# All remainder key tiles at the start of a visit: moving norms, loads and turned pairs forward in a fused attention and MLP kernel

## The chip, the cores and the metric

The kernel runs on one NeuronCore of a Trainium2 chip, as one launch. The metric is the device time of one execution in microseconds (us). TensorE (PE in the profile) multiplies matrices, ScalarE (ACT) applies functions, VectorE (DVE) does elementwise work, GpSimd (POOL) does squares and issues some DMAs, and SyncE (SP) issues the other DMAs, one after the other in the order of the program.

## The reference

```python
# q, k, v: [8 batches, 12 heads, 448 rows, 64]; tau = 0.1
q_n = q / (norm(q) + 1e-6);  k_n = k / (norm(k) + 1e-6)
attn = softmax(q_n @ k_n.T / tau);  o = attn @ v
x = o.transpose(0, 2, 1, 3).reshape(8 * 448, 768)   # heads side by side
h = x @ w_in                     # [3584, 2048]
out = max(0.01 * h, h) @ w_out   # [3584, 768]
```

## The kernel before

**Pairs.** The heads of a batch are taken two at a time: six pairs a batch, 48 pairs in all, numbered s. For a pair, `load_qk(s)` (L135) issues four DMAs on SP: two of 192 KB for rows 0 to 383 of q and of k, and two small ones for the 64 remainder rows. `squares(s)` (L171) squares them on POOL, `sums(s)` (L184) reduces them on DVE, `roots(s)` (L195) takes Ln and Exp on ACT, and `normalise(s)` (L211) divides on DVE and leaves bf16 `qn[s]`. `transposes(s)` (L246) then turns `qn[s]`, so that the head dimension lies on the partitions: `qkT[s]`, here called the turned pair. From pair 10 on this is one transposing DMA on SP (L252); before, PE and DVE do it. `norm(s)` (L690) is the bundle: roots, normalise, the turn, the load of a later pair (s + 4), a small copy `hold` on POOL (L509) that makes POOL wait for `qn[s]`, and the squares of pair s + 2.

**Key tiles.** `key_tiles` (L265) multiplies the keys of a pair with its queries. A pair has three full tiles of 128 key rows (ki = 0 to 2). The 64 remainder rows of two neighbouring pairs share one more tile (ki = 3), named by the odd pair of the two; it reads both turned pairs. So a batch has 18 full tiles and three remainder tiles: pairs 0 and 1, 2 and 3, 4 and 5. Each takes two of the eight PSUM banks until ACT has taken the exponent of it (L289) into `pe` (full) or `pr` (remainder).

**Stages.** After a start-up for batch 0 the loop at L759 runs over chunks b = 0 to 7 of token rows, with 384 rows in even chunks and 512 in odd ones. For each of them:

1. *visit b* (`visit`, L718) multiplies chunk b by w_out, in `groups` (L437) of three or four blocks of 128 rows, and deals out the 21 key tiles of batch b + 1 between the steps of it. A step is one pair of half-depth matmuls that run side by side; a block has 32 steps. The dictionaries `three`, `four` and `wide` (L735 to L737) say after which step how many tiles come. Two remainder tiles stand ahead of the first block (L723), the third behind the last (L733).
2. `attend_batch(b + 1)` (L679) forms softmax sums and products with v for the three pairs of pairs, two of these together (`attend_two`) and then one (`attend`), and scales them into `xT`.
3. `firsts(b + 1, ...)` (L708), here the *first stage* of chunk b + 1, multiplies by w_in: 16 slices m of six matmuls each, 384 columns wide in even chunks and 512 in odd ones. Each is followed on ACT by the leaky ReLU into `hT` (L388).

PE thus goes visit 1, attend 2, first stage 2, visit 2 and so on, and only the last chunk has no key tiles.

**What sets the order.** All of it is written by hand: each engine takes its instructions in the order in which the program names them. The dictionaries `norms` (by block and step in a visit) and `between` (by m in a first stage) name the places of the norms and sums. `ready` counts the pairs whose norms are placed. A visit's batch need not be all turned at its start: a pair is turned at the latest shortly before its own tiles come. With batch b + 1 due in visit b, the last two or three pairs of the batch have their norms in the visit itself.

**Buffers.** raw q and k of the first six pairs and of pairs 10 and 11 lie in `raw0`; the others rotate through four `ld` buffers. Turned pairs rotate through five `qt` buffers. The weights `w_out` come in four DMAs on POOL's queue, two behind `norm(6)` and two behind `norm(7)`.

Of the kernel before, what the change touches and what calls it, by code (L numbers as in the profile page):

```python
# [8 lines left out]
F32 = mybir.dt.float32  # L9
# [7 lines left out]
def kernel(  # L17
# [11 lines left out]
    B, H, S, D = q.shape  # L29
# [7 lines left out]
    NPAIR = H // 2  # L37
    NSLOT = B * NPAIR
    NQ = NPAIR // 2
# [8 lines left out]

    ctx.enter_context(tc.manual_schedule())
    cpool = ctx.enter_context(tc.tile_pool(name="consts", bufs=1))  # L50
    ldp = ctx.enter_context(tc.tile_pool(name="ld", bufs=4))
    vbp = ctx.enter_context(tc.tile_pool(name="vb", bufs=4))
    sqp = ctx.enter_context(tc.tile_pool(name="sq", bufs=3))
    smp = ctx.enter_context(tc.tile_pool(name="small", bufs=3))
    qnp = ctx.enter_context(tc.tile_pool(name="qn", bufs=3))
    qtp = ctx.enter_context(tc.tile_pool(name="qt", bufs=5))
    pep = ctx.enter_context(tc.tile_pool(name="pe", bufs=6))
    prp = ctx.enter_context(tc.tile_pool(name="pr", bufs=3))
    rbp = ctx.enter_context(tc.tile_pool(name="rb", bufs=2))
# [50 lines left out]
    def load_w_out(parts):  # L110
        for m in parts:
            gp.dma_start(out=w_out_sb[:, m : m + MT // 4], in_=w_out_r[:, m : m + MT // 4])

    def main(x, b, h0, nh):
        return x[b, h0 : h0 + nh, 0:MAIN].rearrange("h (p t) d -> p h t d", t=3)

    raw0 = cpool.tile([128, NPAIR, 2, 7, D], F32, name="raw0")
    raw = {s: (raw0[:, s, :, 0:4], raw0[:, s, :, 4:7]) for s in range(NPAIR)}

    def load_first(eng, x, part, s0, n):  # L120

        h0, i = 2 * s0, 0 if x is q else 1
        if part == 0:
            dst = raw0[:, s0 : s0 + n, :, 4 * i : 4 * i + 3]
            eng.dma_start(
                out=dst.rearrange("p s h t d -> p (s h) t d"), in_=main(x, 0, h0, 2 * n)
            )
        else:
            dst = raw0[64 * i : 64 * i + 64, s0 : s0 + n, :, 3]
            eng.dma_start(  # L130
                out=dst.rearrange("p s h d -> p (s h) d"),
                in_=x[0, h0 : h0 + 2 * n, MAIN:S].rearrange("h p d -> p h d"),
            )

    def load_qk(s):  # L135
        if s >= NSLOT:
            return
        b, h0 = s // NPAIR, 2 * (s % NPAIR)
        both = raw0[:, s - 10] if s in (10, 11) else ldp.tile([128, 2, 7, D], F32, name="qk")
        nc.sync.dma_start(out=both[:, :, 0:3], in_=main(q, b, h0, 2))  # L140
        nc.sync.dma_start(out=both[:, :, 4:7], in_=main(k, b, h0, 2))
        for i, x in enumerate((q, k)):
            nc.sync.dma_start(
                out=both[64 * i : 64 * i + 64, :, 3],
                in_=x[b, h0 : h0 + 2, MAIN:S].rearrange("h p d -> p h d"),
            )
        raw[s] = (both[:, :, 0:4], both[:, :, 4:7])
# [117 lines left out]
    def key_tiles(which):  # L265

        tiles = []
        for s, ki in which:
            sc = banks(2)
            tiles.append(sc)  # L270
            for i in range(2 if ki == 3 else 1):
                x = qkT[s - 1 + (i ^ s // 2 % NQ % 2)] if ki == 3 else qkT[s]
                for a in range(2):
                    rows = slice(64 * a, 64 * a + 64)
                    out = sc[64 * i : 64 * i + 64] if ki == 3 else sc
                    c0, c1 = (448, 512) if ki == 3 else (512 + 128 * ki, 640 + 128 * ki)
                    nc.tensor.matmul(  # L277
                        out=out[:, a, :S], lhsT=x[rows, c0:c1], rhs=x[rows, 0:S],
                        start=True, stop=True,
                    )  # L280
        for (s, ki), sc in zip(which, tiles):
            if ki == 3:
                pr[s // 2] = prp.tile([128, 2, S], BF16, name="pr")
                dst = pr[s // 2]
            else:
                if s not in pe:
                    pe[s] = pep.tile([128, 3, 2, S], BF16, name="pe")
                dst = pe[s][:, ki]
            nc.scalar.activation(out=dst, in_=sc[:, :, :S], func=AF.Exp, scale=inv_tau)  # L289

    xT = {}
# [217 lines left out]
    def hold(x):  # L509
        seen = smp.tile([128, 1], F32, name="seen")  # L510
        gp.tensor_copy(out=seen, in_=x)  # L511

    hold(raw0[:, 0, 0, 3, 0:1])
    for x in (q, k):
        load_first(gp, x, 1, 3, 3)
    load_v(0)
# [23 lines left out]
    dst = qtp.tile([128, 7, 128], BF16, name="qkT")  # L540
# [137 lines left out]

    def attend_batch(b):  # L679
        if b == 1:  # L680
            load_qk(14)
            load_qk(15)
            sums(12)
        attend_two(b * NQ)
        if b == 1:
            norm(12)
        attend(b * NQ + 2)


    def norm(s, transposed=True):  # L690
        if s >= NSLOT:
            return
        roots(s)
        normalise(s)
        if transposed:
            transposes(s)
        if s == 10:
            return
        for x in (12, 13) if s == 11 else (s + 4,) if s > 11 else ():
            load_qk(x)  # L700
        hold(qn[s][:, 6, 0, 0:1])
        if s == 11:
            squares(12)
        squares(s + 2)
        if s in (6, 7):
            load_w_out((0, 4) if s == 6 else (8, 12))

    def firsts(b, begun, between):  # L708

# [8 lines left out]
    def visit(b, order, norms, between):  # L718


        s0 = (b + 1) * NPAIR
        tiles = [(s0 + p, ki) for p in range(NPAIR) for ki in range(3)]
        key_tiles([(s0 + 1, 3), (s0 + 3, 3)])  # L723
        for i, pairs in enumerate(order):
            last = i == len(order) - 1
            after = between[last]
            for n, _ in enumerate(groups(b, pairs, 4 if len(pairs) > 1 else 1, last), 1):
                for _ in range(after.get(n, 0)):
                    key_tiles([tiles.pop(0)])
                for fn in norms.get((i, n), ()):  # L730
                    fn()
        assert not tiles
        key_tiles([(s0 + 5, 3)])  # L733

    three = ({5: 1, 11: 1, 16: 2, 21: 1, 27: 1}, {3: 1, 7: 1, 11: 1, 16: 2, 20: 1})  # L735
    wide = (dict.fromkeys((5, 11, 16, 22, 27, 33, 38, 44, 49, 55, 60), 1), dict.fromkeys(range(4, 29, 4), 1))
    four = ({5: 1, 11: 1, 16: 2, 24: 1}, {6: 1, 16: 2})  # L737

    deals["apart"] = False
    attend(NQ - 1, [lambda m=m: first(0, m, range(KT - 2)) for m in range(3, SOON)])  # L740
    behind(nc.sync, scalings[NQ - 1, 0], "weights first")
    load_qk(10)
    load_qk(11)
    norm(6, False)
    norm(7, False)
    firsts(
        0, SOON, {
# [4 lines left out]
            11: [lambda: transposes(8), lambda: load_v(4)],  # L752
            13: [lambda: load_v(5), lambda: load_v_rem(1)],
            14: [lambda: transposes(9), lambda: sums(10)],
            15: [lambda: norm(10)],
        },
    )
    ready = 10
    for b in range(B):  # L759
        tokens = chunk_cols(b)[1] // 128  # L760
        if b == B - 1:
            for ts in range(tokens):
                for half in range(2):
                    second(b, ts, half)
            break
        order = [[((ts, 0), (ts, 1))] for ts in range(tokens)]
        if b == 0:
            order = [order[0] + order[1], order[2]]
        norms = {(0, 8): [lambda: sums(11)], (0, 18): [lambda: norm(11)]}
        if b:  # L770
            norms = {}
            for i in range(tokens - 1):
                norms[i, 4] = [lambda s=ready + i: norm(s)]
                norms[i, 20] = [lambda s=ready + i + 1: sums(s)]
        visit(b, order, norms, wide if b == 0 else three if tokens == 3 else four)
        ready += tokens - 1
        attend_batch(b + 1)
        for j in range((b + 2) * NQ, (b + 3) * NQ):
            load_v(j)
        load_v_rem(b + 2)  # L780
        s = ready
        between = {0: [lambda s=s: norm(s)], 1: [lambda s=s: sums(s + 1)]}
        if b == 0:
            between = {
                0: [lambda: sums(13)], 1: [lambda: norm(13), lambda: sums(14)],
                4: [lambda: norm(14), lambda: sums(15)], 7: [lambda: norm(15)],
                13: [lambda: sums(16)],
            }
            ready += 4
        elif tokens == 3:  # L790
            between.update({
                4: [lambda s=s: norm(s + 1), lambda s=s: sums(s + 2)],
                7: [lambda s=s: norm(s + 2), lambda s=s: sums(s + 3)],
                10: [lambda s=s: norm(s + 3)], 13: [lambda s=s: sums(s + 4)],
            })
            ready += 4
        else:
            between.update({
                4: [lambda s=s: norm(s + 1)], 5: [lambda s=s: sums(s + 2)],
                8: [lambda s=s: norm(s + 2)], 12: [lambda s=s: sums(s + 3)],  # L800
            })
            ready += 3
        firsts(b + 1, 0, between)


# [33 lines left out]
```

## Time and profile before

| | |
|---|---|
| median of 3 runs | 409.8 us (409.0 to 410.4) |
| the profiled execution | 409.4 us |
| its span, first to last instruction | 407.6 us |
| outside the span | 1.8 us |
| visit 1, with its 21 key tiles | 99.0 to 124.1 us |
| first stage 3 | 173.0 to 193.8 us |
| visit 3 | 193.8 to 218.8 us |

Busy shares of the span: PE 98%, ACT 65%, PEld 53%, DVE 47%, POOL 34%. "PEld" is the load of weights into TensorE, which overlaps the matmuls. Rows of the timeline give the start of a run of equal instructions, its length and how many there are; SPq is the sequencer of SP, whose rows are the issues of DMAs. The transfer itself goes on after the row's end until it lands.

### The profile page before, as it was taken

The page shows a single profiled execution, that of the slowest core. Times are in us where ns is not written, and L with a number is a line of the kernel's source. Part 1 is how long each engine was busy: PE and PEld are TensorE (multiplying, and loading weights), DVE is VectorE, ACT ScalarE, POOL GpSimd, SP SyncE. Part 2 cuts the span into 40 slices and gives each one's busy share as a digit, 9 for nine tenths or more (in the row PEclk, how much of TensorE's full clock was granted, in tenths as well). Part 3 has the DMA queues.
Part 4 walks back from the last instruction along what each step waited for, and adds up shares of the span by engine and source line. Part 5 has one row for each costly group of instructions (what it writes and reads, how often), then busy time and mean ns, then how long its engine had stood idle before and what let it go on. Part 6 is the DMA issues. An engine that isn't in the chain of part 4 may idle for free.

```text
span 407.6 us, 10141 instructions
## 1 busy us (share of the span) xinstructions
PE 399.9 (98%) x4096; PEld 215.1 (53%) x4096; DVE 189.6 (47%) x405; ACT 263.1 (65%) x454; POOL 138.7 (34%) x212
## 2 busy tenths in 40 slices
PE   7999999999999999999999999999999999999996
PEld 2335566544555655544555555544555555554564
DVE  6987941770644624354542635256261645130021
ACT  5996498565865589745876569845876559944300
POOL 4973842371323432253241614055231530000000
PEclk9999999999999999999999999999999999999999
DMA  7999999596497848377396957486378833210033
GB/s 187 247 214 240 202 200 223 160 192 120 107 189 127 146 82 216 65 117 179 71 168 149 130 121 165 111 117 145 84 177 157 111 75 63 63 41 2 0 78 78
DMA packets 102095, 54.21 MB, mean 133 GB/s; under 512 B 69984, under 2 KB 96992, under 8 KB 102048
## 3 DMA queue, kind: packets, MB, share of 16 engines
q1 hardware_dynamic: 78064, 41.04, 43.9%
q0 software_dynamic: 23136, 12.00, 22.4%
q8 instruction: 32, 0.52, 0.5%
q10 hardware_dynamic: 848, 0.52, 0.4%
q14 instruction: 15, 0.12, 0.1%
HBM read 45.61 MB, written 11.01 MB: 139 GB/s over the span
## 4 chain that ended last, share of the span: by engine, by line
PE 88%; DVE 5%; POOL 2%; ACT 1%; DMA 1%; issue 1%; POOLq 0%
PE ps L381 33%; PE ps L456 31%; PE ps L317 11%; PE ps L277 8%; PE ps L418 5%; DVE qn L220 2%; PE ps L304 1%; POOL sq L180 1%; DMA raw<-in_k_dram 1%; DVE ss L191 1%; DVE ss L215 1%; DVE qkT L258 1%; DVE r L216 0%; POOL raw L130 0%; POOL v_rem L165 0%
## 5 line engine op out<-in xcount | busy, mean ns | idle before, releaser
L381 PE MATMUL ps<-xT,w_in_sb 128*128 128x384 bf16 (+1 forms) x768 | 148.2, 353 | 0.0
L456 PE MATMUL ps<-w_out_sb,hT 64*128 64x384 bf16 x1536 | 143.4, 323 | 0.0
L289 ACT ACTIVATE pe<-ps 128x896 bf16<-128x896 f32 x144 | 124.0, 918 | 20.0 <-PE ps L277 18.0
L388 ACT ACTIVATE hT<-ps 128x384 bf16<-128x384 f32 (+1 forms) x128 | 67.4, 543 | 70.5 <-PE ps L381 70.2
L381 PEld LDWEIGHTS <-w_in_sb 128*128 128x128 bf16 x768 | 74.1, 98 | 71.9 <-issue 4.0
L456 PEld LDWEIGHTS <-hT 64*128 64x128 bf16 x1536 | 75.0, 94 | 53.9 <-PE ps L456 4.2
L180 POOL TENSOR_TENSOR sq<-qk 128x512 f32<-128x512 f32 x80 | 73.4, 938 | 10.7 <-DMA qk<-in_k_dram 10.1
L277 PE MATMUL ps<-qkT 64*128 64x448 bf16 (+1 forms) x384 | 54.9, 354 | 1.3 <-ACT pr L289 0.5
L468 DVE COPY osb<-ps 128x384 f32<-128x384 f32 x41 | 21.2, 553 | 74.6 <-PE ps L456 44.1
L511 POOL CAST seen<-qn 128x1 f32<-128x1 bf16 x47 | 8.8, 186 | 136.0 <-DVE qn L220 127.2
L191 DVE TENSOR_REDUCE ss<-sq 128x6 f32<-128x384 f32 (+1 forms) x95 | 54.4, 611 | 1.2 <-POOL sq L180 1.1
L220 DVE TENSOR_TENSOR qn<-qk,r 128x512 bf16<-128x512 f32 x80 | 48.2, 644 | 1.7 <-DVE r L216 0.3
L215 DVE TENSOR_SCALAR ss<-ss 128x14 f32<-128x14 f32 x48 | 10.5, 220 | 69.2 <-ACT ss L199 69.1
L358 DVE TENSOR_TENSOR xT<-ps,rb 128x448 bf16<-128x448 f32 x48 | 27.8, 620 | 26.6 <-ACT rb L337 26.4
L158 POOL DMA_DIRECT2D v_b<-in_v_dram x24 | 18.6, 776 | 54.2 <-PE ps L317 54.2
L317 PE MATMUL ps<-pe,v_b 128*32 128x448 bf16 x576 | 32.0, 353 | 0.0
L277 PEld LDWEIGHTS <-qkT 64*128 64x128 bf16 (+1 forms) x384 | 16.6, 96 | 20.6 <-issue 8.5
L424 DVE COPY osb<-ps 128x384 f32<-128x384 f32 (+1 forms) x9 | 4.6, 514 | 36.6 <-issue 22.6
L317 PEld LDWEIGHTS <-v_b 128*32 128x32 bf16 x576 | 15.2, 97 | 11.9 <-issue 0.6
L289 ACT ACTIVATE pr<-ps 128x896 bf16<-128x896 f32 x24 | 21.3, 920 | 0.2 <-PE ps L277 0.2
L336 ACT ACTIVATE rb<-ps 128x448 f32<-128x448 f32 x24 | 12.9, 538 | 13.1 <-PE ps L317 12.1
L418 PE MATMUL ps<-w_out_sb,hT 128*128 128x384 bf16 (+1 forms) x144 | 21.0, 308 | 0.0
(49 smaller groups left out, 204.4 us busy)
## 6 DMA issues: line engine op xcount, KB each, us to landing
qk<-in_q_dram SPq DMA_DIRECT2D x40, 192.0 KB, 3.2
qk<-in_k_dram SPq DMA_DIRECT2D x40, 192.0 KB, 3.3
out_dram<-osb SPq DMA_DIRECT2D x30, 192.0 KB, 2.8
v_b<-in_v_dram POOLq DMA_DIRECT2D x24, 192.0 KB, 4.9
out_dram<-osb SPq DMA_DIRECT2D x12, 384.0 KB, 2.7
w_in_sb<-in_moe_w_in_dram POOLq DMA_DIRECT2D x4, 768.0 KB, 12.3
w_out_sb<-in_moe_w_out_dram POOLq DMA_DIRECT2D x4, 768.0 KB, 11.3
raw<-in_q_dram SPq DMA_DIRECT2D x8, 192.0 KB, 4.8
```

The source lines that it names most:

```text
L180: eng.tensor_tensor(sq, x, x, op=ALU.mult)
L191: nc.vector.tensor_reduce(o.rearrange("p (h t) -> p h t", h=2), sqs[s][i], axis=AX.X, op=ALU.add)
L220: scalings[s] = nc.vector.tensor_tensor(qn[s][:, lo:hi], x.rearrange("p h t d -> p t h d"), r[:, r0 : r0 + 2 * nt].rearrange("p (h t) -> p ...
L277: nc.tensor.matmul(out=out[:, a, :S], lhsT=x[rows, c0:c1], rhs=x[rows, 0:S], start=True, stop=True,)
L289: nc.scalar.activation(out=dst, in_=sc[:, :, :S], func=AF.Exp, scale=inv_tau)
L317: nc.tensor.matmul(out=x[32 * g : 32 * g + 32, :S], lhsT=weights(g, ki) if ki < 3 else rem(g), rhs=pe[s][:, ki, a, :] if ki < 3 else pr[j] ...
L358: scalings[j, e] = nc.vector.tensor_tensor(xT[m][:, 2 * jj + e, half * S : (half + 1) * S], pos.pop((j, e))[:, :S], rbs[j], op=ALU.mult,)
L381: nc.tensor.matmul(out=pm[:, :n], lhsT=w_in_sb[:, kt, m * 128 : (m + 1) * 128], rhs=xT[c // 2][:, kt, c0 : c0 + n], start=(kt == 0), stop= ...
L388: nc.scalar.activation(out=hT[c][:, m, :n], in_=pms.pop((c, m))[:, :n], func=AF.Prelu, alpha=0.01)
L418: nc.tensor.matmul(out=po2[:, :n], lhsT=hT[c][:, m, ts * 128 : (ts + 1) * 128], rhs=w_out_sb[:, m, lo : lo + n], start=(m == 0), stop=(m = ...
L456: done[p][i] = nc.tensor.matmul(out=pos2[p][:, i, :HALF], lhsT=hT[c][rows, m, ts * 128 : (ts + 1) * 128], rhs=w_out_sb[rows, m, half * HAL ...
L468: copy(out=osb[c, ts][:, half * HALF : (half + 1) * HALF], in_=po2[:, i, :HALF])
```

## The change

- All six slots of `raw0` (now `raw_sb`) are used round for all pairs (pair s in slot s mod 6), the four `ld` buffers go, and `qt` has seven buffers in place of five. `norm(s)` loads pair s + 6 in place of s + 4. For this the loads of pairs 14 to 17 stand together in `attend_batch(1)`, where those of 14 and 15 stood.
- From visit 1 on, the third remainder tile stands with the other two at the visit's start. So all six pairs of a batch have to be turned before the visit begins. For odd b, norms of three pairs stand in visit b, and three in the first stage after it (m = 0, 4, 8). For even b from 2, a visit has none: one norm stands in `attend_batch`, and five in the first stage after it (m = 1, 4, 7, 9, 11, with the sums one m ahead).
- The 18 full tiles stand one at a time, some 4 to 6 steps apart, where before some came in twos.
- `norm(10)` moves from the end of first stage 0 to step 3 of visit 0. The first of the four `w_out` DMAs is issued earlier, behind a `hold` on `xT`, the second behind `norm(7)` and the last two behind `norm(8)`.

The number of instructions on each engine stays what it was, but for one `hold` more.

```diff
-    ldp = ctx.enter_context(tc.tile_pool(name="ld", bufs=4))
-    qtp = ctx.enter_context(tc.tile_pool(name="qt", bufs=5))
+    qtp = ctx.enter_context(tc.tile_pool(name="qt", bufs=7))
...
-        both = raw0[:, s - 10] if s in (10, 11) else ldp.tile([128, 2, 7, D], F32, name="qk")
+        both = raw_sb[:, s % NPAIR]
...
     def attend_batch(b):
         if b == 1:
-            load_qk(14)
-            load_qk(15)
+            for s in range(14, 18):
+                load_qk(s)
             sums(12)
         attend_two(b * NQ)
-        if b == 1:
-            norm(12)
+        if b % 2:
+            norm((b + 1) * NPAIR)
         attend(b * NQ + 2)
...
-        for x in (12, 13) if s == 11 else (s + 4,) if s > 11 else ():
+        for x in (12, 13) if s == 11 else (s + NPAIR,) if s > 11 else ():
             load_qk(x)
...
-        if s in (6, 7):
-            load_w_out((0, 4) if s == 6 else (8, 12))
+        if s in (7, 8):
+            load_w_out((4,) if s == 7 else (8, 12))
...
-        key_tiles([(s0 + 1, 3), (s0 + 3, 3)])
+        key_tiles([(s0 + 1, 3), (s0 + 3, 3)] + [(s0 + 5, 3)] * (b > 0))
...
-        key_tiles([(s0 + 5, 3)])
+        if b == 0:
+            key_tiles([(s0 + 5, 3)])
...
-    three = ({5: 1, 11: 1, 16: 2, 21: 1, 27: 1}, {3: 1, 7: 1, 11: 1, 16: 2, 20: 1})
-    four = ({5: 1, 11: 1, 16: 2, 24: 1}, {6: 1, 16: 2})
+    three = (at(8, 12, 16, 21, 26, 31), at(4, 8, 12, 16, 21, 26, 30), at(3, 8, 12, 16, 20))
+    four = (at(9, 16, 22, 28), at(4, 10, 16, 22, 28), at(4, 10, 16, 22, 28), at(4, 10, 16, 20))
...
+    hold(xT[0][:, 2 * NQ - 2, 0:1])
+    load_w_out((0,))
     norm(6, False)
...
-            15: [lambda: norm(10)],
...
+        s = (b + 2) * NPAIR
+        norms = {}
+        if b == 0:
+            norms = {
+                (0, 3): [lambda: norm(10)], (0, 8): [lambda: sums(11)],
+                (0, 18): [lambda: norm(11)],
+            }
+        elif b % 2:
+            for i in range(3):
+                norms[i, 4] = [lambda x=s + i: norm(x)]
+                norms[i, 20] = [lambda x=s + i + 1: sums(x)]
...
+        between = {}
+        for i, m in enumerate((0, 4, 8) if b % 2 else (1, 4, 7, 9, 11)):
+            x = s + i + (3 if b % 2 else 1)
+            between.setdefault(m, []).append(lambda x=x: norm(x))
+            if b % 2 == 0:
+                between.setdefault(max(m - 1, 0), []).insert(0, lambda x=x: sums(x))
+        if b % 2:
+            for i, m in enumerate((2, 6, 12)):
+                between[m] = [lambda x=s + 4 + i: sums(x)]
         else:
+            between[14] = [lambda x=s + NPAIR: sums(x)]
         firsts(b + 1, 0, between)
```

## The prediction

> **What bounds the kernel now.** I read the page's busy shares and its chain first, then the PE timeline at a visit's two ends, then SP's.
>
> ```profile
> PE 399.9 (98%) x4096; PEld 215.1 (53%) x4096; DVE 189.6 (47%) x405; ACT 263.1 (65%) x454; POOL 138.7 (34%) x212
> ...
> PE 88%; DVE 5%; POOL 2%; ACT 1%; DMA 1%; issue 1%; POOLq 0%
> ```
>
> PE is busy for 98% of the span and is 88% of the chain that ended last; from 51 us on the chain is almost PE alone. So two things alone move the time: what PE streams, and any wait of PE. First stage 3 has 96 matmuls of 512 columns from 172.95 to 193.77 us, 0.217 us each and nothing between. In visit 1 the last 32 matmuls run as 16 pairs of 0.1625 us. PE's rows at the start and the end of visit 1:
>
> ```profile
> 99.00 0.57 PE L277 MATMUL ps<-qkT 64*64 64x448 bf16 x8
> 99.50 0.99 PE L456 MATMUL ps<-w_out_sb,hT 64*128 64x384 bf16 x10
> ...
> 121.12 2.76 PE L456 MATMUL ps<-w_out_sb,hT 64*128 64x384 bf16 x32
> 123.81 0.38 PE L277 MATMUL ps<-qkT 64*64 64x448 bf16 x4
> 124.13 0.38 PE L304 MATMUL ps<-pr,ones 64*32 64x448 bf16 x8
> ```
>
> Take starts, not lengths, which overlap. The 16 pairs need 2.60 us from 121.12, to 123.72, but the remainder tile starts at 123.81: 0.09 us when the shape of the array's part changes. A tile's four matmuls run together, 0.19 us (448 columns at the rate above), yet the next shape starts 0.32 us later: 0.13 us for that change. At the start two tiles take 0.50 us to the next shape, two times 0.19 and 0.12. These changes are all that PE loses in visits 1 to 6. There is little to win, so the question is what the new order makes PE wait for.
>
> **Part 1, the remainder tile moved.** The tile's 0.19 us are paid in either place. At the end, two changes (0.09 and 0.13) become one, straight from the groups to the products. No row shows that change; a change of shape takes 0.09 to 0.13 us everywhere here, so it saves 0.09 to 0.13 a visit, less 0.03 for a third tile beside the two. I take 0.08 us, six times: **-0.5** (-0.4 to -0.6).
>
> **Part 2, tiles spaced evenly.** A tile among the groups costs no more than its columns (100.33 to the next group's start at 100.52 is 0.19), so single or double is the same to PE: 0. That holds while ACT keeps up. An exponent takes 0.83 to 0.92 us; four steps and a tile take PE 0.84. A three-block visit has 21 exponents, 18 us, in 20 us, and loses its roots, so ACT hides. Before the first full tile, which comes at step 8 or 9, three remainder tiles and the products fill all eight banks; its banks are free when the first exponent ends, some 1.5 us in, and it comes 2.0 us in. If that cover fails, each late tile costs tenths of a us.
>
> **Part 3, `norm(10)` to step 3 of visit 0.** At 52.33 us PE waits 0.34 us beyond a step for banks that `pr` frees: on ACT the roots of pair 10 stand ahead of those exponents, 51.04 to 51.59. Now they stand behind: **-0.3** (0 to -0.34). The turned pair 10 is then issued near 55.1, not 53.4, and at the 8.6 us that it took lands at 63.7; its first tile comes near 65.5. The last two `w_out` DMAs are issued 3.8 us later (behind `norm(8)`), but the first starts over 4 us earlier, and they follow each other at 3.8 to 4.0 us by their landings (47.8, 51.6, 55.3, 59.3). Their slices are read from about 57.9 and 61.1 us on. Cover of 2 us each; I take 0.
>
> **Part 4, all six pairs turned before a visit.** This is the step that decides. It changes what must be ready when visits 1, 3 and 5 begin, after a first stage that now holds five norms. Pair 17 (29, 41) comes last. SP's rows in first stage 3:
>
> ```profile
> 181.05 1.26 SPq L252 DMA_TRANSPOSE qkT<-qn  x1
> 182.41 0.53 SPq L140 DMA_DIRECT2D qk<-in_q_dram  x1
> 182.99 0.47 SPq L141 DMA_DIRECT2D qk<-in_k_dram  x1
> 183.51 0.63 SPq L143 DMA_DIRECT2D qk<-in_q_dram  x1
> 184.18 0.60 SPq L143 DMA_DIRECT2D qk<-in_k_dram  x1
> 184.93 1.77 SPq L252 DMA_TRANSPOSE qkT<-qn  x1
> ```
>
> A turn holds SP's queue 1.26 us, the load behind it 2.37, with gaps 3.74 us; 0.11 us later the next turn can go. So one norm takes **3.85 us of SP's queue**, however early its data are. (Behind loads some turns take longer: 1.47, 1.77 and 1.82 us.) The same tile view for this stretch tells how long a turned pair takes from issue to landing:
>
> ```profile
> L252 SPq DMA_TRANSPOSE qkT<-qn x4: 1254/1256/1772, 175.4 to 189.3; - x4
> DMA to landing us min/median/max: 2.9/3.0/3.4
> ```
>
> In first stage 3 the second norm of the batch (pair 25) stands at m = 1; its roots wait on ACT behind the first leaky ReLU. In first stage 1, where the kernel has a norm at that place already, that ReLU starts at 81.41 and the turn at 84.19, 2.78 us later; here it starts at 176.11, so the turn goes at 178.9. Four more periods of SP put the turn of pair 29 at 178.9 + 4 x 3.85 = 194.3, and its landing at 197.25 with 2.95 us. PE comes to the third remainder tile at 193.77 + 2 x 0.21 = 194.2. PE takes its instructions in order, so the whole visit stands behind that tile. The wait is 3.05 us at least; I add 0.35 for one slow turn in two visits and for landings of 3.1: **+3.4** in visit 3 and the same in visit 5, whose stage has the same rows 94.7 us later. The upper end is 5.5: four periods of 4.36 (one slow turn in each) and a landing of 3.4.
>
> The norms alone would be late too. On DVE the sums of pair 14 start at 84.04 and those of the next, behind its norm, at 87.90:
>
> ```profile
> 84.04 1.14 DVE L191 TENSOR_REDUCE ss<-sq 128x8 f32<-128x512 f32 x2
> 85.80 0.42 DVE L215 TENSOR_SCALAR ss<-ss 128x14 f32<-128x14 f32 x1 [0.62 <-ACT ss L199]
> 86.25 0.24 DVE L216 RECIPROCAL r<-ss 128x14 f32<-128x14 f32 x1
> 86.53 1.45 DVE L220 TENSOR_TENSOR qn<-qk,r 128x512 bf16<-128x512 f32 x2
> 87.90 1.14 DVE L191 TENSOR_REDUCE ss<-sq 128x8 f32<-128x512 f32 x2
> ```
>
> Sums, two roots on ACT (0.62 us idle), norm: 3.86 us, and 3.3 to 3.6 where POOL's squares don't slow them. So m = 7, 9, 11 (2.6 us apart) are not kept; the last norm ends near 192.2, and its turn would land at 195.1.
>
> Visit 1 is worse, as SP has loads 14 to 17 in one row before turn 12. The two that were there run from 72.48 to 78.02 (2.26 and 3.17 us); two more at 2.8 end at 83.6, so turn 12, whose data are ready at 78.3, waits 5 us. Five periods later, at 102.9, goes turn 17; with 0.45 for the slow turns of this stretch (1.47 and 1.82) and 3.3 to landing it is there at 106.65. PE wants it at 99.43: **+7.2**. Bounds: loads of 2.4 and landing in 2.9 give 5.7; loads of 3.2, periods of 4.36 and a landing of 4.4 give 11.4.
>
> Visits 2, 4 and 6 don't wait: their last turn stays at m = 8 (141.58 in first stage 2, landing 3.0 us later) against 146.9. The loads into used slots wait for nothing: their readers ended long before.
>
> **Sum.** -0.5 - 0.3 + 7.2 + 3.4 + 3.4 = +13.2 us. The profiled execution took 409.4 (span 407.6), the median is 409.8; I start from the former: **422.6 us**, by the bounds 420 to 431 (-0.9 + 11.7; -0.4 + 22.4).
>
> **Where the Trainium skill says more.** PE would idle for 3 to 7 us, longer than anywhere after the start. The kernel's first 20 warming matmuls take 5.87 us in one row, against 4.5 for 19 starts at 0.217 and one length of 0.38: about 1.4 us for a cold start.
>
> ```profile
> 1.49 5.87 PE L502 MATMUL ps<-warm 128*128 128x512 bf16 x20 [1.49 <-DVE warm L485]
> ```
>
> Whether an idle of 3 to 7 us makes PE cold again, no row shows. The Trainium skill, "TensorE: Matmul & The Clock Gate", section "Part 1: The HAM clock gate", says that an idle window of about 3.4 us halves TensorE's clock until a busy window has passed. By that rule visit 1 would surely start cold, and visits 3 and 5 perhaps.
>
> **Rivals.**
> - *PE starts cold after each wait* (0.25): 1.4 us each, one to three times, 424.0 to 426.8; I put 425. For it: the cold row at the start. Against: the granted clock is 0.999 throughout.
> - *SP is not what binds; the norms are* (0.09): loads issue faster than their rows say. Then turn 17 goes when its norm ends, near 98.4, and lands at 101.35, 1.9 late; in visits 3 and 5 0.9 each: -0.8 + 3.7, 412.3. Against: 3.85 us between turns comes back wherever SP is full.
> - *No wait, not slower* (0.04): the last turn lands before the third tile. From 194.2 back, it must be issued by 191.2, 3 us sooner than the sum; even an SP that is full from the turn of pair 24 on, at 173.0, gets to 192.3. What is left is parts 1 and 3: 408.6.
> - *Weights late in visit 0* (0.04): the last `w_out` DMAs keep their 3.8 us delay and eat the 2 us of cover: 2 us twice, up to 426.6.
>
> The forecast itself has 0.58. **Range 417 to 430**: it holds the forecast but for its far upper end, the cold starts and the late weights, and leaves out the two rivals below. About 1.2 us, 0.3%, is what a measurement can tell from no change. **Chances**: slower 0.95 (forecast, cold starts, norms, weights), same 0.03, faster 0.02 (of the rival without a wait, which lies at the edge).
>
> **What would show it.** Right: PE idle ahead of the remainder tiles (L276 in the new file) in visits 1, 3 and 5, ended by the DMA of `qkT`, 7 us and two times 3.4; SP rows without gaps from 72 to 103 us; turns 3.85 us apart; none of that in visits 2, 4, 6; PE's other rows as before. Wrong: waits that end on ACT in a visit (spacing), a wait ahead of the groups of visit 0 (weights), steps of 0.32 us behind a wait (cold), or turns closer than 3.85 us.

## The result, and the profile after

The changed kernel takes 435.3 us (median of 6 runs, 434.7 to 438.1) against 409.2 for the kernel before (409.0 to 410.4): 1.064 times as long, 95% interval 1.062 to 1.066. Slower was forecast, but by 13 us, to 422.6 with a range up to 430; it is 26 us. The profiled execution took 438.1 us with a span of 436.4. It is the longest of the six, so its terms below add up to 28.8 us (the difference of the spans) rather than 26.

Four lines of the page after: the busy shares, the clock granted in 40 slices, the chain by engine, and the key tiles' group with its idle time.

```profile
PE 411.0 (94%) x4086; PEld 225.7 (52%) x4096; DVE 194.4 (45%) x405; ACT 265.1 (61%) x454; POOL 139.6 (32%) x213
...
PEclk9999999997799999999699999999889999999999
...
PE 75%; DMA 11%; DVE 5%; POOL 4%; SPq 3%; ACT 1%; issue 1%; POOLq 0%
...
L276 PE MATMUL ps<-qkT 64*128 64x448 bf16 (+1 forms) x384 | 62.1, 362 | 17.8 <-DMA qkT<-qn 16.4
```

PE's share of the chain falls from 88 to 75%, and transfers and SP's queue take 14%. PE now idles 17.8 us ahead of key tiles, 16.4 of them ended by the DMA that brings a turned pair. And the clock row, all nines before, has three dips: visits 1, 3 and 5.

PE's timeline lets the execution be cut at the first matmul of each stage. Lengths in us:

| stage | before | after | difference |
|---|---|---|---|
| up to visit 0 | 51.16 | 51.82 | +0.66 |
| visit 0 | 20.43 | 20.62 | +0.19 |
| visit 1 | 25.13 | 36.81 | +11.68 |
| visit 3 | 25.13 | 33.34 | +8.21 |
| visit 5 | 25.13 | 32.50 | +7.37 |
| visits 2, 4, 6, each | 19.93 | 20.27 | +0.34 |
| attends behind visits 1 to 6, each | 6.56 | 6.48 | -0.08 |
| first stages, each | 15.7 or 20.8 | the same | 0 |

The sum is 0.66 + 0.19 + 11.68 + 8.21 + 7.37 + 1.02 - 0.48 = 28.65 us. The first row can't be put down to the change: visit 0 starts between 50.9 and 52.3 us in the nine traces with the changed start, and at 51.2 and 51.9 us in the two with the old one.

PE at the start of visit 3, after:

```profile
206.43 0.57 PE L276 MATMUL ps<-qkT 64*64 64x448 bf16 x8
208.49 0.38 PE L276 MATMUL ps<-qkT 64*64 64x448 bf16 x2 [1.49 <-DMA qkT<-qn]
212.33 0.58 PE L276 MATMUL ps<-qkT 64*64 64x448 bf16 x2 [3.46 <-DMA qkT<-qn]
212.84 3.06 PE L455 MATMUL ps<-w_out_sb,hT 64*128 64x384 bf16 x18
```

Two remainder tiles run; the third waits twice, for pair 28 and for pair 29. By starts, less 0.40 for the two tiles and 0.19 for the half tile that run in between, that is 1.66 and 3.65 us, 5.3 in all. In the same way visit 5 loses 4.3 and visit 1 8.1 us, together **17.7 us of waits**. In visit 1 the second tile waits as well, for pair 15 (0.70 us idle in the timeline), before the third waits for pairs 16 and 17 (3.38 and 3.24 us). The fourth line shows a second loss: nine pairs of matmuls in 2.85 us (from 212.84 to the next tile at 215.69) are 0.32 us a pair, where 0.1625 is usual. The windows view of this stretch (columns: stretch and its length, then busy us and instructions of PE, PEld, DVE, ACT and POOL, then the granted clock, the DMA engines' share and GB/s):

```profile
206.00:213.00 7.00, 2.05 (x17) 0.51 (x17) 1.57 (x4) 2.71 (x5) 2.01 (x3) 0.79 0.74 173
213.00:217.00 4.00, 4.00 (x28) 1.79 (x26) 2.59 (x6) 1.96 (x4) 0.86 (x2) 0.51 0.19 55
217.00:225.00 8.00, 8.00 (x96) 5.05 (x94) 2.59 (x8) 5.75 (x9) 1.15 (x2) 1.00 0.56 137
```

PE is busy for all of 213 to 217, at a granted clock of 0.51. So after the wait it runs at half speed for some 4 us. Cut finer, the windows view puts the half clock at 104.3 to 114.6, 210.1 to 217.0 and 312.5 to 319.4 us: 10.2, 6.8 and 6.8 us, each begun while PE still waits.

A third loss is small and in the blocks of visits 1 to 6 (all but the first of visit 1, which runs at half clock there). Two timelines at step 16 of a block, first the kernel before (two tiles there), then the changed one (one tile):

```profile
149.88 0.54 PE L277 MATMUL ps<-qkT 64*128 64x448 bf16 x4
150.26 0.97 PE L456 MATMUL ps<-w_out_sb,hT 64*128 64x384 bf16 x10
```

```profile
162.53 0.35 PE L276 MATMUL ps<-qkT 64*128 64x448 bf16 x2
162.88 0.99 PE L455 MATMUL ps<-w_out_sb,hT 64*128 64x384 bf16 x10
```

Two tiles take 0.38 us from start to the next start; one takes 0.35 and not 0.19. Between steps 16 and 17 `groups` has an explicit wait of PE (`behind`) for the products of the other rows in the same banks; the matmul of step 16 must have ended, which a second tile covers and one does not. That this wait is the cause is read from the code; that one tile at step 16 costs the time and two do not is tested in e5 and e2.

### The profile page after: what moved, and what is told of

It reads as the page before. It is cut to its first block, busy times and chain, and to the rows that moved or that the text cites. A ratio compares the mean times of both kernels' runs of the same rounds, so it can differ in the third digit from the quotient of the medians.

```text
span 436.4 us, 10172 instructions
## 1 busy us (share of the span) xinstructions
PE 411.0 (94%) x4086; PEld 225.7 (52%) x4096; DVE 194.4 (45%) x405; ACT 265.1 (61%) x454; POOL 139.6 (32%) x213
## 3 DMA queue, kind: packets, MB, share of 16 engines
q0 software_dynamic: 23136, 12.00, 21.1%
## 4 chain that ended last, share of the span: by engine, by line
PE 75%; DMA 11%; DVE 5%; POOL 4%; SPq 3%; ACT 1%; issue 1%; POOLq 0%
PE ps L455 29%; PE ps L380 24%; PE ps L316 9%; PE ps L276 6%; DMA qkT<-qn 5%; PE ps L417 5%; DMA w_in_sb<-in_moe_w_in_dram 3%; DVE qn L219 2%; DMA raw_sb<-in_k_dram 2%; POOL sq L179 2%; SPq L142 1%; DVE ss L190 1%; PE ps L303 1%; DVE ss L214 1%; POOL v_rem L164 1%
## 5 line engine op out<-in xcount | busy, mean ns | idle before, releaser
L455 PE MATMUL ps<-w_out_sb,hT 64*128 64x384 bf16 x1536 | 154.8, 333 | 0.0
L288 ACT ACTIVATE pe<-ps 128x896 bf16<-128x896 f32 x144 | 127.6, 920 | 28.3 <-PE ps L276 26.3
L455 PEld LDWEIGHTS <-hT 64*128 64x128 bf16 x1536 | 84.8, 97 | 53.8 <-issue 9.1
L387 ACT ACTIVATE hT<-ps 128x384 bf16<-128x384 f32 (+1 forms) x128 | 65.7, 542 | 55.0 <-PE ps L380 54.1
L179 POOL TENSOR_TENSOR sq<-raw_sb 128x512 f32<-128x512 f32 x92 | 85.2, 948 | 12.8 <-DMA raw_sb<-in_k_dram 11.9
L276 PE MATMUL ps<-qkT 64*128 64x448 bf16 (+1 forms) x384 | 62.1, 362 | 17.8 <-DMA qkT<-qn 16.4
L219 DVE TENSOR_TENSOR qn<-raw_sb,r 128x512 bf16<-128x512 f32 x96 | 58.7, 652 | 2.8 <-DMA qkT<-qn 0.7
L214 DVE TENSOR_SCALAR ss<-ss 128x14 f32<-128x14 f32 x48 | 13.5, 282 | 55.2 <-ACT ss L198 55.1
L276 PEld LDWEIGHTS <-qkT 64*128 64x128 bf16 (+1 forms) x384 | 18.6, 98 | 36.8 <-DMA qkT<-qn 19.2
L197 ACT ACTIVATE ss<-ss,tiny 128x14 f32<-128x14 f32 x48 | 14.5, 302 | 22.5 <-DVE ss L190 21.9
```

The source lines that it names most:

```text
L179: eng.tensor_tensor(sq, x, x, op=ALU.mult)
L219: scalings[s] = nc.vector.tensor_tensor(qn[s][:, lo:hi], x.rearrange("p h t d -> p t h d"), r[:, r0 : r0 + 2 * nt].rearrange("p (h t) -> p ...
L276: nc.tensor.matmul(out=out[:, a, :S], lhsT=x[rows, c0:c1], rhs=x[rows, 0:S], start=True, stop=True,)
L387: nc.scalar.activation(out=hT[c][:, m, :n], in_=pms.pop((c, m))[:, :n], func=AF.Prelu, alpha=0.01)
L455: done[p][i] = nc.tensor.matmul(out=pos2[p][:, i, :HALF], lhsT=hT[c][rows, m, ts * 128 : (ts + 1) * 128], rhs=w_out_sb[rows, m, half * HAL ...
```

## The experiments

The theory after the result, called *late turns*, has three terms: waits for turned pairs that SP brings too late (17.7 us), TensorE at half clock behind each long wait, and the uncovered wait at step 16. For the second, visit 3 leaves 8.21 - 5.31 - 4 x 0.155 (the uncovered wait, 0.343 us for a tile and not 0.189, in each of four blocks) + 0.08 (the tile's place) = 2.4 us; visits 1, 3 and 5 together about 8. The rivals were that the crowded schedule hurts without the tile, that the slow pairs are late operands, that the spacing is harmless, and that the norms, not SP, set the turns.

**e1, e2: the tile put back.**

```diff
-        key_tiles([(s0 + 1, 3), (s0 + 3, 3)] + [(s0 + 5, 3)] * (b > 0))
+        key_tiles([(s0 + 1, 3), (s0 + 3, 3)])
...
-        if b == 0:
-            key_tiles([(s0 + 5, 3)])
+        key_tiles([(s0 + 5, 3)])
# e2 alone, besides:
+    three = (at(5, 11, 16, 16, 21, 27), at(5, 11, 16, 16, 21, 27), at(3, 7, 11, 16, 16, 20))
+    four = (at(5, 11, 16, 16, 24),) * 3 + (at(6, 16, 16),)
```

> The changed kernel with only the third remainder tile put back behind the last group of every visit. Late turns theory: the 17.7 us of waits in visits 1, 3 and 5 are all for the turned pairs of that one tile, and the 8.2 us of slow matmuls behind them come from the waits; both go, and what stays is 21 blocks with one key tile at step 16 in place of two, 0.137 us each, 2.9 us: 412.2 us against 409.2. Rival, the crowded schedule itself (loads in one row, five norms in a stage) makes other tiles wait as well: 415 us or more, with waits of PE on turned pairs left.

> As e1, and the key tiles dealt out as in the kernel before, two of them after step 16. Spacing theory: the second tile at step 16 hides PE's own wait for the other rows' products of the same bank, so the 2.9 us go too: 409.4 us (what is left of the change: start-up, weights, loads). Rival, the 0.14 us at step 16 comes from the order of the banks or from ACT, not from the single tile: 412 us, like e1.

Measured: e1 413.6 us, 1.0095 times the kernel before (1.008 to 1.011); e2 411.2 us, 1.0037 (1.002 to 1.005). So 22 of 26 us hang on the place of one tile, and the pairs at step 16 are worth 2.3 us more, near the 2.9 expected. Both are over the number by 1.4 to 1.8 us, and not all waits went: visit 1 is 26.5 us long in both, and its second remainder tile waits for pair 15. PE in e2:

```profile
98.54 0.38 PE L276 MATMUL ps<-qkT 64*64 64x448 bf16 x4
100.17 0.38 PE L276 MATMUL ps<-qkT 64*64 64x448 bf16 x4 [1.24 <-DMA qkT<-qn]
```

That is the rival's part: loads 14 to 17 in one row on SP make turn 15 late as well, by 1.4 us. The first turn behind them, of pair 12, goes at 84.44 us in the changed kernel and at 78.32 in the kernel before.

**e3: the waits filled.**

```diff
-        key_tiles([(s0 + 1, 3), (s0 + 3, 3)] + [(s0 + 5, 3)] * (b > 0))
+        key_tiles([(s0 + 1, 3), (s0 + 3, 3)])
+        if b in (1, 3, 5):
+            fill({1: 24, 3: 16, 5: 12}[b])
+        if b > 0:
+            key_tiles([(s0 + 5, 3)])
```

> The changed kernel with 24, 16 and 12 extra matmuls on constant data (0.217 us each) between the second and the third remainder tile of visits 1, 3 and 5, shorter than the waits there; their results are not used. Clock theory: the 8.2 us behind the waits, matmul pairs of 0.32 us in place of 0.16, are TensorE cold after more than 3 us without work; with the wait filled no idle is over 3 us, the slow pairs go and the time is 427 us. Rival, the slow pairs come from operands or banks that arrive late after the wait: 435 us, with the slow pairs in place.

Measured: 428.2 us (1.046; 1.044 to 1.049), 7 us less than the changed kernel, for 52 matmuls more. Visit 3 in this trace, and its windows row:

```profile
203.59 3.63 PE L501 MATMUL ps<-warm 128*128 128x512 bf16 x16
207.15 0.38 PE L276 MATMUL ps<-qkT 64*64 64x448 bf16 x2
207.88 0.38 PE L276 MATMUL ps<-qkT 64*64 64x448 bf16 x2 [0.35 <-DMA qkT<-qn]
208.19 0.99 PE L455 MATMUL ps<-w_out_sb,hT 64*128 64x384 bf16 x10
```

```profile
203.00:212.00 9.00, 8.65 (x75) 4.01 (x76) 3.46 (x9) 5.16 (x9) 2.52 (x5) 1.00 0.55 136
```

The tile still waits for pair 29, but the groups behind it run five pairs in 0.82 us and the clock stays 1.00. The slow pairs come from the idle time, not from operands. This also measures them: from the third tile's last matmuls to the end of the visit, visits 1, 3 and 5 take 28.14, 27.45 and 27.58 us in the changed kernel and 25.24 here, so half clock costs 2.9, 2.2 and 2.3 us, 7.4 in all. The rest of the 8 us is 0.19 us a visit for the third tile, whose halves a wait parts where they otherwise run together.

**e4: loads out of the way of the turns.**

```diff
+        held = s > 11 and s % 12
+        if held not in (1, 2, 3, 4):
+            for x in (12, 13) if s == 11 else range(s + 2, s + 7) if held == 5 else (s + NPAIR,) if s > 11 else ():
+                load_qk(x)
```

> The changed kernel with four loads of each crowded first stage (those that follow its second to fifth norm) moved on SP behind the stage's last turn. SP queue theory: SP's queue sets the turns, and without the loads only the norms on DVE and ACT do, one each 3.6 us: the last turn of visits 3 and 5 is issued some 2.7 us earlier, near 2.6 us of wait in place of 5.3 and 4.3, too short for a cold start; visit 1 keeps about 4 us. Some 422 us. Rival, the norms set the turns and the queue only follows: waits stay within 1 us of what they were, 433 us or more.

Measured: 427.0 us (1.041; 1.037 to 1.044). SP now turns pairs 25 to 29 as fast as the norms come, the issues starting 3.97 and then 3.66 us apart, and the last turn goes 20.96 us after the start of first stage 3, where it was 23.73. Visits 3 and 5 wait 2.5 us each, as expected from 2.6, and visit 1 4.3. The queue was the bound, and behind it stand the norms, still too late. What was missed is the clock. The five turns on SP, then PE in visit 3 and the windows behind the wait:

```profile
186.97 16.17 SPq L251 DMA_TRANSPOSE qkT<-qn  x5
```

```profile
201.78 0.76 PE L276 MATMUL ps<-qkT 64*64 64x448 bf16 x10
204.85 0.38 PE L276 MATMUL ps<-qkT 64*64 64x448 bf16 x2 [2.32 <-DMA qkT<-qn]
```

```profile
202.00:204.80 2.80, 0.53 (x10) 0.10 (x2) 0.91 (x2) 2.10 (x3) 0.17 (x1) 1.00 0.51 91
204.80:208.00 3.20, 3.15 (x22) 1.56 (x24) 1.27 (x4) 1.32 (x3) 0.65 (x1) 0.60 0.75 213
```

Even 2.3 us without a matmul, behind 0.8 us of 64 by 64 tiles, were enough for the clock to fall to 0.60 over the next 3.2 us. Cut finer, the half clock lies at 205.5 to 208.9 us, so it begins after PE is back at work. It makes the rest of visits 3 and 5 1.7 and 1.5 us longer than in e3, 3.2 of the 5 us between 422 and 427. Such a wait need not halve the clock: one of the four executions took 423.4 us at a mean granted clock of 0.991, where the others have 427 us at 0.984. By an estimate from these, 0.007 of 424 us, it spent some 6 us less at half clock, near the two stretches of 3.4 us; no trace of it is kept.

**e5: the spacing alone, in the kernel before.** It takes the dictionaries `three` and `four` of the changed kernel, and `after = between[i]`.

> The kernel before, with the changed kernel's places for the full key tiles alone: one at a time, with one at step 16. Spacing theory: each of the 21 blocks of visits 1 to 6 shows 0.14 us more between the tile at step 16 and the next group, 2.9 us in all: 412.1 us against 409.2. Rival, evenly spaced tiles are kinder to ACT and nothing else changes: 409 us or less.

Measured: 413.1 us, 1.0088 times (1.0076 to 1.010). Visits 1, 3 and 5 are 0.62 us longer, visits 2, 4 and 6 0.47: 3.3 us for 21 blocks, and step 16 looks as it does in the changed kernel:

```profile
103.05 0.35 PE L277 MATMUL ps<-qkT 64*128 64x448 bf16 x2
103.40 1.15 PE L456 MATMUL ps<-w_out_sb,hT 64*128 64x384 bf16 x12
```

The new spacing is a loss by itself, and all of it lies at step 16: a single tile at any other step takes 0.19 us in this trace, as before.

**e6: v loads first.** The hold and the squares behind `norm(24)` and `norm(36)` go behind the loads of v. The edit does the same to those behind `norm(12)`, ahead of visit 1.

> The changed kernel with the hold and the squares that follow the norm in attend 3 and attend 5 put behind the loads of v on POOL's queue, where the kernel before has them. Collision theory: in the changed kernel the v loads of first stages 3 and 5 start some 14 us after those of the kernel before, into the turns, and stretch SP's periods from 3.85 to 4.3 and 5.8 us; with them earlier the waits of visits 3 and 5 fall from 5.3 and 4.3 to 3.4 us each: 432.5 us. Rival, the long periods have another cause: 435 us and the same periods.

Measured: 436.4 us (431.0 to 437.4), no gain; the ratio to the kernel before is 1.063 (1.057 to 1.068). The waits of visits 3 and 5 did fall, to 4.2 and 3.4 us, and those of visit 1 rose from 8.1 to 8.6. The period between turns 25 and 26 is back at 3.85, but the next is 5.09, with one load's issue of 1.78 us. So the v loads are a part of the long periods; what the rest is stays open.

**e7, e8, e9: time for the turns.** e7 has the third tile first from visit 2 on and catches up in visit 1; e8 from visit 3 on, catching up in visits 1 and 2; e9 is e8 with the third tile last everywhere. All keep two tiles at step 16. The core of e8:

```diff
+        key_tiles([(s0 + 1, 3), (s0 + 3, 3)] + [(s0 + 5, 3)] * (b > 2))
...
+        elif b in (1, 2):
+            x0 = 16 if b == 1 else 23
+            for i in range(tokens):
+                norms[i, 4] = [lambda x=x0 + i: norm(x)]
+                norms[i, 20] = [lambda x=x0 + i + 1: sums(x)]
+        else:
+            for i in range(tokens - 1):
+                norms[i, 4] = [lambda x=s + i: norm(x)]
+                norms[i, 20] = [lambda x=s + i + 1: sums(x)]
```

> A version that gives the turned pairs their time: visit 1 keeps the third tile last and holds five norms (24 us of room), visits 3 and 5 three, 2, 4 and 6 two, and the first stages three or four, the places of the kernel before but two pairs ahead from visit 2 on; the third tile stands first from visit 2 on, and two tiles stay at step 16. Late turns theory: no wait for a turned pair is left, and what is won is one change of shape in each of five visits, about 0.08 us each: 408.8 us, no measurable difference to 409.2. Rival, the first place is worth more than that (the last exponents no longer run beside attend): 407 us or less; or ACT, with three remainder tiles ahead, makes PE wait: 411 us or more.

> As e7, with the catching up spread out: visit 1 four norms, visit 2 three, first stages 2 and 3 three and four, and the third tile first only from visit 3 on. In e7 visits 3 to 6 and the attends were shorter than in the kernel before by some 0.8 us in all, and visits 1 and 2, which had five norms and a late pair 23, longer by 2.2. Late turns theory: with time for every turn the 2.2 go and the 0.8 stay: 408.3 us against 409.1, faster by 0.2%, at the edge of what can be told. Rival, one norm more in a visit costs PE what the tile's place gives, through ACT: 409 us or more.

> As e8, but the third remainder tile last in every visit: it has the same norms, loads and turns, and tells what the tile's place alone is worth. One change of shape less in each of visits 3 to 6 (0.08 us, and as much again in the attend behind it by e7's trace): e8 shorter than e9 by 0.3 to 0.7 us. Rival, the place is worth nothing once the turns are early: e8 and e9 within 0.2 us.

Measured: e7 410.9 us (1.0043; 1.002 to 1.006), e8 409.15 (0.9997; 0.9985 to 1.0009), e9 409.97 (1.0007; 0.9994 to 1.002). e7 missed: pair 23 came 1.4 us late in visit 2, and visit 1 with five norms is 0.75 us longer. In e8 no visit waits. Its visits 3 and 5 take 25.05 us against 25.13, visits 4 and 6 19.80 against 19.93, and the attends behind them 6.48 against 6.56: 0.74 us in the trace. All of that is the tile's place, since in e9, with the same norms, these lengths are those of the kernel before to 0.01 us. PE at the end of visit 3 in e8, where the products follow the groups directly:

```profile
217.28 1.51 PE L455 MATMUL ps<-w_out_sb,hT 64*128 64x384 bf16 x16
218.72 0.38 PE L303 MATMUL ps<-pr,ones 64*32 64x448 bf16 x8
```

e8 was expected at 408.3 us, and shorter than e9 by 0.3 to 0.7. Over the runs that gain can't be told from none; e8 beats the changed kernel by 26 us and the kernel before by nothing that is clear of noise.

## Why the prediction was wrong

**The tile moved (-0.5): right.** About 0.08 us a visit was forecast. e8 against e9 shows 0.08 in visits 3 and 5 and 0.13 in 4 and 6, and 0.08 more in the attend behind, which I had not counted. The change from groups to products, of which no row told, takes 0.14 us in e8: the eight pairs from 217.28 need 1.30 us, and the products start at 218.72.

**Tiles spaced evenly (0): wrong, +3.3 us (e5).** The step read the price of a tile among the groups from the one place where nothing waits, 100.33 us, and concluded that two in a row or one are the same to PE. It looked for a cover that ACT might lose and not for one that PE has: the second tile at step 16 hid PE's own wait for a bank. That wait stands in the code, as `behind(nc.tensor, ...)`, and the trace before shows nothing of it exactly because it was covered. Elsewhere the step held: a single tile at any other step costs its 0.19 us, and in no visit of the changed kernel from 1 on does PE wait for an exponent.

**`norm(10)` in visit 0 (-0.3, cover 2 us): near.** Visit 0 is 20.24 to 20.26 us against 20.43 in seven of the nine traces with the new start, -0.18 (20.42 in e3). In the profiled execution of the changed kernel it is 20.62: turn 10 took 10.4 us to land, not 8.6, the cover was gone, and PE waited 0.34 us for its tile.

**Turned pairs (+14.0): right in mechanism and place, 17.7 us in size.** Visit 1: 7.2 forecast, 8.1 measured; visits 3 and 5: 3.4 each, 5.3 and 4.3. The first turn went where the sum had it: 191.62 us, or 6.0 after the stage's start, as in the forecast's 178.9 less 172.9. The mis-sized term is four periods of 3.85 us; SP in first stage 3:

```profile
191.62 1.27 SPq L251 DMA_TRANSPOSE qkT<-qn  x1
...
195.88 1.98 SPq L251 DMA_TRANSPOSE qkT<-qn  x1
...
199.30 1.59 SPq L142 DMA_DIRECT2D raw_sb<-in_q_dram  x1
...
201.64 1.26 SPq L251 DMA_TRANSPOSE qkT<-qn  x1
...
205.49 1.26 SPq L251 DMA_TRANSPOSE qkT<-qn  x1
...
209.34 1.26 SPq L251 DMA_TRANSPOSE qkT<-qn  x1
```

The periods are 4.26, 5.76, 3.85 and 3.85, 17.7 us where the sum had 15.4; the five periods before visit 1 take 21.1, where it had 19.7. Issues of the same DMAs take longer (1.98 for a turn, 1.59 for a small load) in the stretch where transfers land late, the first two turns 7.1 and 6.4 us after their issue and the last three 2.9 to 3.0. The upper end of the forecast, 5.5 for a visit, holds them.

**PE cold after each wait: a rival at 0.25, and it came true.** The text held against it that the granted clock is 0.999 throughout; that was no evidence, as PE had no such idle time before. Its price was too low as well: 1.4 us, from the cold start of the warming matmuls, against 2.2 to 2.9 us each (e3). The half clock lasted 2.8 us at the kernel's start and 4.6 to 6.0 us from PE's return in the changed kernel. Its stretches in the traces are 3.4 us (e4), 6.8 and 10.2 us long, which is once, twice and three times 3.41 us. That suggests that the clock is set anew in fixed steps, and that where a step falls has a part in whether a short wait is followed by half clock; no run here tests it. The Trainium skill's page "TensorE: Matmul & The Clock Gate", section "Part 1: The HAM clock gate", has a half clock follow an idle window of about 3.4 us and last until a busy window has passed. The order and the 3.4 us agree with the stretches, but the window need not be idle throughout: in e4 2.3 us without a matmul sufficed.

Taken together: 17.7 waits, about 8 cold (with the 0.6 for the parted tile), 3.3 spacing, less 1.1 for the tile's place and attends, with 0.2 in visit 0 and 0.7 at the start, is 28.8, the difference of the spans. The forecast had 13.2, so 15.6 are missing in this execution. The failed step is the sum itself, which left the cold starts to a rival and the spacing at nothing: about 11 of the 15.6 us are these two. Another 3.7 are the turned pairs, whose periods on SP were taken at their usual length.

## What to carry to other kernels

When work is moved to an earlier place, count what its inputs cost on the slowest queue from the point where they can start, as here 3.85 us of SP for each pair; a place that saves 0.1 us can ask for data that are 5 us away. Count an idle PE twice: the wait and, where it lasts 2.3 us or more as here, the time at half clock after it, which filling matmuls avoid. And before work is taken out of a row, look in the code for waits that it covers, since a trace shows none that is covered.

## What the runs showed of the hardware that was not expected

- 2.3 us without a matmul, behind 0.8 us of small tiles, halved the clock (0.60 over the next 3.2 us; e4, in three of four executions by their mean clock), while a remaining gap of 1.7 us did not (e3, visit 1: 1.00).
- Back from a wait, TensorE ran at half speed for 4.6 to 6.0 us, though it was busy all the while (0.51 over 213 to 217 us), and the stretches at half clock were 3.4, 6.8 or 10.2 us long.
- SP's issue of one and the same load of 192 KB took between 0.37 and 1.6 us in the changed kernel, and a turn 1.22 to 2.4 us; a period on a full queue varied from 3.85 to 5.76 us.
- A change from groups to products takes 0.14 us (e8), and a wait for the other rows' products in a bank is uncovered by 0.155 us behind one key tile and covered behind two (e5 and e2).
